# Delta rule and Fourier mixing: unread matrix products between the products of two recurrence steps and behind the first mixed tile

## The chip, the core and the metric

The kernel runs on one core of a Trainium2 chip. TensorE (PE in the profile, its weight loads PEld), VectorE (DVE), ScalarE (ACT) and GpSimd (POOL) each work through a queue of their own in order; SyncE (SP) and POOL issue the DMAs. The metric is the device time of one execution in microseconds (us), lower is better, given as a median of runs. One further execution was taken with the hardware profiler; all rows come from it.

## The reference

Two blocks in a row, all in float32. First a delta rule over 4 batches, 8 heads, 768 steps and a head size of 48:

```
k_n = k / (norm(k) + 1e-6)
for t in range(S):
    y[t]  = q[t] @ state
    v_old = state^T k_n[t]
    state = state + beta[t] * outer(k_n[t], v[t] - v_old)
```

Its output, with the 8 heads side by side (384 columns), is the input x of the second block:

```
mixed = real(fft(fft(x, axis=1), axis=2))
u  = x + mixed
un = (u - mean(u)) / sqrt(var(u) + 1e-6)
out = u + relu(un @ w_ch1) @ w_ch2        # 384 -> 1536 -> 384
```

The weights arrive as float64.

## The kernel before

The recurrence is done in chunks of 64 steps, 12 chunks (`NCH`) to a batch, 48 in all; chunk `m` belongs to batch `m // 12`. A chunk is a call of `chain(m)`, a generator with three stages. The first multiplies the state into the keys (`pc<-st,KQT` in the trace) and lets DVE take the difference `U` from the values; the second applies the chunk's inverted triangle (`pc<-U,wt`), which ACT copies back to `U`; the third adds the chunk to the state (`pc<-U,kp`, then `st<-st,pc` on DVE), and is left out for a batch's last chunk (`if n < NCH - 1`). `outputs` forms the rows of y for a pair of chunks (`py`) and puts them into the tiles `x`, six tiles of 128 rows to a batch, held as three pairs. `prepare` transposes keys and queries (`pt`, then ACT to `KQT`) and forms their products (`pg`); `invert` inverts the triangles on DVE (`A`, `X`), `merge` joins their blocks (`pj`).

`fourier(b)` mixes a batch: `folded` and `shifted` form sums on DVE (`hT`, `F` of the first batch), a product with the table `stab` transforms along the rows (`pf`, read back by ACT into `F` and `gz`), and for each of three tile pairs `T` a product with `dtab` transforms along the columns (`pb`), after which six DVE sums add it to `x[T]`; the last pair has four further sums (`pd`). Mean and variance follow on DVE, the root on POOL (`rstd`). `mlps` normalises (`un`), transposes (`ptr`, `unT`), and does the two products of the last block (`ph`, then ACT to `hT`; `po`, then DVE into `x`).

The float64 weights are turned into float32 on the chip: a DMA brings a tile into one of `x_149`, `x_150`, `x_151` (still free), two ACT passes and two DVE passes split it, and POOL joins it into `w`. The second weight's twelve tiles (`second_weight`) are under way while batch 0 is mixed.

The order of the work is that of the calls, with a planner behind it. Up to `m = 11` the order is written out by hand and kept (`strict[0] = True`). From `m = 12` on it is not: a loop with due times (`PRE`, `SIDE`) mixes `chain`, `prepare`, `invert`, `mlps` and `fourier`, and a scheduler sets the final order on each engine. Results of TensorE go through PSUM tiles. Those that `ps_one` hands out (`pt`, `pf`, `pb`, `pd`, `ph`, `po`, `ptr`) share two slots:

```
def ps_one(shape, name):
    return ps.tile(shape, F32, tag="one", bufs=2, name=name)
```

so each waits until the one two places ahead of it has been read. In the profiled execution chunk 11 begins at 143.7 us, chunk 12 at 154.3 us, and the sums of tile pairs 0, 1 and 2 of batch 0 at 167.4, 178.0 and 187.6 us. A matrix product of the program is two records in the trace. Line 131 in the profile is the helper that issues the calls of DVE, ACT and TensorE, so groups are told apart by tile names.

Of the kernel before, what the change touches and what calls it, by code (L numbers as in the profile page):

```python
# [82 lines left out]
def kernel(  # L83
# [15 lines left out]
    NCH = S // CH  # L99
# [17 lines left out]
    def ps_pair(name, tag):  # L117
        return ps.tile([128, 2, 512], F32, tag=tag, name=name)

    def ps_one(shape, name):  # L120
        return ps.tile(shape, F32, tag="one", bufs=2, name=name)
# [18 lines left out]
    def mm(o, lhsT, rhs, start, stop=True):  # L140
        return pe.matmul(o, lhsT=lhsT, rhs=rhs, start=start, stop=stop, skip_group_check=True)
# [48 lines left out]
    def loads():  # L190


        while at["k"] < min(len(quads), at["chain"] + len(kps)):
            load(at["k"], 0)
        while at["q"] < min(len(quads), at["prepare"] + len(qps)):
            load(at["q"], 1)
# [10 lines left out]
    def values(Q):  # L207
        vals[Q] = wk.tile([128, QT, 4, D], F32, tag="V4", bufs=2, name="V4")
        b, i = quads[Q]
        n = QT * i  # L210
        mid = min(max(NCH // 2 - n, 0), QT)
        for cs in (slice(0, mid), slice(mid, QT)):
            w = cs.stop - cs.start
            t0 = (n + cs.start) * CH + (1 if cs.start < mid else 0)
            for p in range(2):
                for u in range(4):
                    if w:
                        eng = nc.gpsimd if NW <= Q + 1 < 5 and p else nc.sync
                        eng.dma_start(out=vals[Q][64 * p:64 * p + CH, cs, u, :],
                                      in_=v[b, 4 * (p ^ (u % 2)) + u, t0:t0 + w * CH, :].rearrange(  # L220
                                          "(c p) d -> p c d", p=CH))

    def scaled(Q):

        if Q in vals and Q in lengths:
            vf = vals[Q].rearrange("p c u d -> p (c u) d")
            ln = lengths.pop(Q)
            dve.tensor_tensor(vf, vf, ln[:, :, None].broadcast_to([128, QT * 4, D]), op=ALU.mult)
# [11 lines left out]
    stab = const.tile([128, 1281], F32, name="stab")  # L240
# [406 lines left out]
    def first_state(b):  # L647
        xs[b] = [xpairs[i] for i in OF_BATCH[b]]
        v0m = wk.tile([NBH, H, D], F32, tag="un", bufs=2, name="v0m")
        dve.tensor_tensor(v0m, v0[:, None, :].broadcast_to([NBH, H, D]),  # L650
                          ident[0:NBH, H * b:H * b + H, None].broadcast_to([NBH, H, D]), op=ALU.mult)
        p0 = ps_one([128, 2 * 2 * D], "p0")
        for e in range(2):
            mm(p0[64 * e:64 * e + 64], k0, v0m.rearrange("p (j e) d -> p e j d", e=2)[:, e], True)
        dve.tensor_copy(sts[NCH * b % 3].rearrange("p h x -> p (h x)"), p0)

    def chain(m):


        b, n = divmod(m, NCH)  # L660
        Q, c = divmod(m, QT)
        KQT, kp, LQ = held[Q]
        if c == 0:
            scaled(Q)
        V4 = vals[Q]
        wt = wts[Q % NW]
        st, nst = sts[m % 3], sts[(m + 1) % 3]
        if n == 0 and b > 0:
            first_state(b)
        pc = ps_pair("pc", "ch")  # L670

        pk = pc[:, :, 0:2 * D].rearrange("p e (j d) -> p e j d", j=2)
        for j in range(2):
            for hh, e in ((0, 0), (1, 1), (0, 1), (1, 0)):
                pr = slice(64 * e, 64 * e + D)
                o = 64 * (hh ^ e)
                mm(pk[o:o + 64, e, j], KQT[pr, c, j, hh, 0, :], st[pr, hh, D * j:D * j + D], True)
        U = wk.tile([128, 4, D], F32, tag="U", bufs=4, name="U")
        ue = "p (j e) d -> p e j d"
        dve.tensor_tensor(U.rearrange(ue, e=2), V4[:, c].rearrange(ue, e=2), pk, op=ALU.subtract)  # L680
        yield

        pu = pc[:, :, 4 * D:6 * D].rearrange("p e (j d) -> p e j d", j=2)
        for j in range(2):
            for e in range(2):
                for hh in range(2):
                    pr = slice(64 * (hh ^ e), 64 * (hh ^ e) + 64)
                    mm(pu[64 * hh:64 * hh + 64, e, j], wt[pr, c, 2 * j + e], U[pr, 2 * j + e], True)
        act.activation(U.rearrange(ue, e=2), pu, ACT.Copy)
        yield  # L690
        if c == 0:
            at["chain"] = Q
            loads()
            if Q + 1 < len(quads) and Q + 1 not in vals:
                values(Q + 1)
        if c == 1:
            held.pop(Q - 1, None)

        if n < NCH - 1:
            pS = pc[:, :, 2 * D:4 * D]  # L700
            for j in range(2):
                for hh, e in ((0, 0), (1, 1), (0, 1), (1, 0)):
                    pr = slice(64 * hh, 64 * hh + 64)
                    mm(pS[64 * e:64 * e + 64, hh, D * j:D * j + D], kp[pr, c, 2 * j + e, :], U[pr, 2 * j + e], True)
            dve.tensor_tensor(nst, st, pS, op=ALU.add)
        pair[n % 2] = c, KQT, LQ, st, U
        if n % 2 == 1:
            later.append(outputs(b, n, *pair))
        if c == QT - 1:
            scaled(Q + 1)  # L710
        yield
# [65 lines left out]
    def fourier(b):  # L777

        x = xs[b]
# [80 lines left out]
        def add(dst, src, op):  # L860
            dve.tensor_tensor(dst, dst, src, op=op)

        for T in range(TH):
            pb = ps_one([128, DM], "pb")
            ts = slice(128 * T, 128 * T + 128)
            mm(pb[:, 0:HD + 1], F[:, 0, 0, ts], dtab[:, 0, 0:HD + 1], True)
            mm(pb[:, 0:HD + 1], F[0:HD - 127, 0, 1, ts], dtab[0:HD - 127, 1, 0:HD + 1], False)
            mm(pb[:, HD + 1:DM], F[:, 1, 0, ts], dtab[:, 0, HD + 1:DM], False)
            mm(pb[:, HD + 1:DM], F[0:HD - 129, 1, 1, ts], dtab[0:HD - 129, 1, HD + 1:DM], False)
            add(x[T][:, :, 0:HD + 1], pb[:, None, 0:HD + 1].broadcast_to([128, 2, HD + 1]), ALU.add)  # L870
            add(x[T][:, :, HD + 1:DM], pb[:, None, HD - 1:0:-1].broadcast_to([128, 2, HD - 1]), ALU.add)
            for t, op in enumerate((ALU.subtract, ALU.add)):
                rop = ALU.add if op == ALU.subtract else ALU.subtract
                add(x[T][:, t, 1:HD], pb[:, HD + 1:DM], op)
                add(x[T][:, t, HD + 1:DM], pb[:, DM - 1:HD:-1], rop)
            yield
            if T == TH - 1:

                pd = ps_one([128, DM], "pd")
                q3 = slice(96, 128)  # L880
                mm(pd[q3, 0:HD + 1], gz[:, 0, :], dtab[:, 0, 0:HD + 1], True)
                mm(pd[q3, 0:HD + 1], gz[0:HD - 127, 1, :], dtab[0:HD - 127, 1, 0:HD + 1], False)
                for t, op in enumerate((ALU.subtract, ALU.add)):
                    add(x[T][q3, t, 0:HD + 1], pd[q3, 0:HD + 1], op)
                    add(x[T][q3, t, HD + 1:DM], pd[q3, HD - 1:0:-1], op)
                yield
            mv = wk.tile([128, GT, 2], F32, tag="mv", bufs=NC // GT, name="mv")
            for tt in range(GT):
                bst = wk.tile([128, 6], F32, tag="bst", bufs=2, name="bst")
                dve.bn_stats(bst, x[T][:, tt, :])  # L890
                dve.bn_aggr(mv[:, tt, :], bst)
            rstd = wk.tile([128, GT], F32, tag="rstd", bufs=NC // GT, name="rstd")
            pool.tensor_scalar(rstd, mv[:, :, 1], 1e-6, None, op0=ALU.add)
            pool.tensor_tensor(rstd, rstd, half_n, op=ALU.pow)
            norms[b, T] = mv, rstd
            yield
# [129 lines left out]
    M.diagonal(0, 0)  # L1026
    M.products(1, 0)
    step = chain(0)
    advance(step)
    M.diagonal(0, 1, dve.tensor_copy)  # L1030
# [14 lines left out]
    T = lambda l, step: lambda: merges[l].taken(step)  # L1045
# [9 lines left out]
    key_work = {(7, 0): 2, (8, 2): 3, (9, 0): 1, (10, 2): 2, (11, 0): 1, (11, 1): 2, (11, 2): 1}  # L1055
    rest = seq(w.join(), masks(3))
    first_mixing = fourier(0)
    for m in range(1, NCH):
        if m == 3:
            merges.update({2: Merge(1, 0, crossed=False), 3: Merge(1, 1, crossed=False)})  # L1060
        for i, _ in enumerate(chain(m)):
            if pe_work[m][i]:
                pe_work[m][i]()
# [74 lines left out]
    for m in range(NCH, STEPS):  # L1138
        b, n = divmod(m, NCH)
# [70 lines left out]
```

## Time and profile before

| | us |
|---|---|
| median of 6 runs | 776.62 |
| lowest and highest of them | 774.32, 777.77 |
| the profiled execution | 774.29 |
| its span on the core | 772.6 |
| PE busy | 678.4 (88%) |
| DVE busy | 391.1 (51%) |
| ACT busy | 260.9 (34%) |
| POOL busy | 83.3 (11%) |
| mean granted clock of TensorE | 0.982 |

The span is the time between the first and the last record; 1.7 us lie around it. The busy shares say which engine has the most work over the whole, and not which one a stage waits for: for that, the rows of the stage are read in order of time.

### The profile page before, as it was taken

To read this page: it belongs to the slowest core of one execution; us is meant where nothing else is said; L and a number is where in the kernel's file an instruction comes from. 1 tells how busy PE (TensorE), PEld (TensorE's weight loads), DVE (VectorE), ACT (ScalarE), POOL (GpSimd) and SP (SyncE) were. 2 spreads that over 40 slices of the span, in tenths; PEclk is the share of its full clock that TensorE was granted. 3 is DMA by queue.
4 is the path that set the end of the run, shared out by engine and by line. 5 is a ranking of instruction groups with operands and counts; after the bars stand their busy time and mean duration, and the time that the engine had idled before them with its cause. 6 is when DMAs were issued, how large, how long until landed. Compare 5 with 4: busy or idle time off the path is not lost.

```text
span 772.6 us, 18281 instructions
## 1 busy us (share of the span) xinstructions
PE 678.4 (88%) x7768; PEld 487.0 (63%) x7768; DVE 391.1 (51%) x972; ACT 260.9 (34%) x708; POOL 83.3 (11%) x116
## 2 busy tenths in 40 slices
PE   5934598779989989899998999899999989899996
PEld 4622477667647757566756667566667667577683
DVE  2599776877980299436597113989311125300000
ACT  3742354643335512633403445012622021121120
POOL 8010023323100000001100000111000000100000
PEclk9999999998999999999999999899999999999999
DMA  8642033342210221011201110100000000000000
GB/s 185 164 108 47 6 85 64 87 120 68 45 39 17 50 45 31 14 24 38 39 22 30 19 42 3 31 10 17 8 22 2 22 1 1 21 1 21 10 11 20
DMA packets 81041, 30.78 MB, mean 40 GB/s; under 512 B 75856, under 2 KB 77392, under 8 KB 80960
## 3 DMA queue, kind: packets, MB, share of 16 engines
q1 hardware_dynamic: 76560, 21.92, 13.4%
q0 software_dynamic: 2224, 7.31, 3.0%
q8 instruction: 61, 1.00, 0.5%
q10 hardware_dynamic: 2176, 0.39, 0.3%
q14 instruction: 20, 0.16, 0.1%
HBM read 24.87 MB, written 4.72 MB: 38 GB/s over the span
## 4 chain that ended last, share of the span: by engine, by line
PE 54%; DVE 14%; ACT 4%; issue 2%; SPq 1%; DMA 1%; POOL 1%; POOLq 0%; DVEq 0%; ACTq 0%
PE ph L131 20%; PE po L131 18%; DVE X L131 4%; PE pc L131 3%; DVE A L131 3%; PE pf L131 2%; PE pb L131 2%; DVE x L131 2%; ACT wt L131 2%; PE pg L131 2%; PE pt L131 2%; PE py L131 2%; ACT A L131 1%; PE ptr L131 1%; DVE Z L131 1%
## 5 line engine op out<-in xcount | busy, mean ns | idle before, releaser
L131 PE MATMUL ph<-unT,w 128*128 128x256 f32 x864 | 209.0, 391 | 4.3 <-ACT hT L131 2.7
L131 PE MATMUL po<-w,hT 128*128 128x384 f32 x576 | 208.9, 506 | 0.1
L131 PEld LDWEIGHTS ph<-unT,w 128*128 128x128 f32 x864 | 159.1, 191 | 31.2 <-ACT hT L131 5.9
L131 PEld LDWEIGHTS po<-w,hT 128*128 128x128 f32 x576 | 105.4, 193 | 63.3 <-issue 4.2
L131 ACT ACTIVATE hT<-ph 128x256 f32<-128x256 f32 x144 | 54.9, 382 | 187.7 <-PE ph L131 187.2
L131 DVE TENSOR_TENSOR x<-x,po 128x384 f32<-128x384 f32 x24 | 13.2, 550 | 110.2 <-PE po L131 110.2
L131 PE MATMUL pg<-KQT 48*64 48x64 f32 (+1 forms) x1152 | 45.2, 297 | 7.9 <-ACT KQT L131 5.7
L131 PEld LDWEIGHTS pg<-KQT 48*64 48x64 f32 x1152 | 34.4, 178 | 24.3 <-ACT KQT L131 12.7
L770 POOL DMA_INDIRECT out_dram<-x,rows_hi x12 | 12.4, 1030 | 334.8 <-DVE x L131 175.2
L131 DVE TENSOR_TENSOR U<-V,pc 128x192 f32<-128x192 f32 x48 | 16.7, 349 | 57.0 <-PE pc L131 56.9
L131 ACT ACTIVATE KQT<-pt 128x256 f32<-128x256 f32 (+1 forms) x84 | 33.2, 413 | 29.1 <-PE pt L131 28.0
L131 DVE TENSOR_TENSOR A<-X 128x30 f32<-128x30 f32 (+14 forms) x120 | 41.3, 344 | 3.0
L131 ACT ACTIVATE U<-pc 128x192 f32<-128x192 f32 x48 | 15.9, 331 | 79.1 <-PE pc L131 76.8
L131 DVE TENSOR_TENSOR X<-X,A 128x30 f32<-128x30 f32 (+14 forms) x120 | 40.6, 339 | 2.9
L131 DVE TENSOR_TENSOR st<-st,pc 128x192 f32<-128x192 f32 x44 | 15.4, 351 | 43.7 <-PE pc L131 32.0
L131 PEld LDWEIGHTS pc<-st,KQT 48*64 48x64 f32 x768 | 19.3, 158 | 26.6 <-DVE st L131 16.5
L131 PE MATMUL pc<-st,KQT 48*64 48x48 f32 x768 | 26.0, 253 | 10.8 <-DVE st L131 10.5
L131 PEld LDWEIGHTS pc<-U,wt 64*64 64x64 f32 x768 | 20.6, 158 | 20.3 <-issue 9.2
L131 PE MATMUL pt<-pack,qp 128*128 128x128 f32 x96 | 22.6, 331 | 12.2 <-DMA qp<-in_q_dram 11.4
L131 PE MATMUL pc<-U,wt 64*64 64x48 f32 x768 | 27.4, 253 | 5.7 <-DVE U L131 4.1
L131 ACT ACTIVATE A<-pj 32x128 f32<-32x128 f32 (+1 forms) x76 | 20.7, 273 | 32.9 <-PE pj L131 32.2
L131 DVE TENSOR_TENSOR x<-x,pb 128x191 f32<-128x191 f32 (+1 forms) x72 | 24.8, 414 | 13.1 <-PE pb L131 13.0
(135 smaller groups left out, 843.8 us busy)
## 6 DMA issues: line engine op xcount, KB each, us to landing
x<-in_moe_w_ch_dram SPq DMA_DIRECT2D x14, 384.0 KB, 3.4
qp<-in_q_dram SPq DMA_DIRECT2D x96, 48.0 KB, 2.4
kp<-in_k_dram SPq DMA_DIRECT2D x80, 48.0 KB, 2.4
V<-in_v_dram SPq DMA_DIRECT2D x56, 48.0 KB, 2.3
w<-in_moe_w_ch_dram POOLq DMA_DIRECT2D x6, 384.0 KB, 7.7
x<-in_moe_w_ch_dram POOLq DMA_DIRECT2D x4, 384.0 KB, 7.6
V<-in_v_dram SPq DMA_DIRECT2D x64, 24.0 KB, 2.1
out_dram<-x SPq DMA_DIRECT2D x8, 192.0 KB, 1.9
```

Of the source, the lines that this page charges most:

```text
L131: ins = getattr(self.engine, name)(*args, **kwargs)
L770: nc.gpsimd.indirect_dma_start(out=out.rearrange("b s m -> (b s) m"), out_offset=bass.IndirectOffsetOnAxis(ap=rows_hi[:, i:i + 1], axis=0) ...
```

## The change

`busy(m)` issues a product of 128x128 by 128x384 from the table `stab` into a `ps_one` tile named `idle`, that nothing reads. It is called in `chain` behind the first, the second and the third stage, and acts for `m = 11` and `m = 12`. Since the third call stands inside `if n < NCH - 1`, it is not reached for `m = 11`. So five such products are issued. Two further ones stand in `fourier` behind the six sums of batch 0's tile pair 0; they multiply the freshly summed `x[0]` (128 columns of each of its two tiles) with `stab`. Seven in all. No step of the computation is taken out.

```diff
+    def busy(m):
+        if NCH - 1 <= m <= NCH:
+            unread(stab[:, 0:128])
+
+    def unread(lhsT):
+        mm(ps_one([128, 384], "idle"), lhsT, stab[:, 0:384], True)
+
     def chain(m):
...
         dve.tensor_tensor(U.rearrange(ue, e=2), V4[:, c].rearrange(ue, e=2), pk, op=ALU.subtract)
+        busy(m)
         yield
...
         act.activation(U.rearrange(ue, e=2), pu, ACT.Copy)
+        busy(m)
         yield
...
             dve.tensor_tensor(nst, st, pS, op=ALU.add)
+            busy(m)
...
                 add(x[T][:, t, 1:HD], pb[:, HD + 1:DM], op)
                 add(x[T][:, t, HD + 1:DM], pb[:, DM - 1:HD:-1], rop)
+            if b == 0 and T == 0:
+                for t in range(2):
+                    unread(x[T][:, t, 0:128])
             yield
```

In the instruction order that results, TensorE has one `idle` behind chunk 11's `pc<-st,KQT`, one behind its `pc<-U,wt`, two ahead of chunk 12's `pc<-st,KQT` (behind `p<-v0m,k`, the batch's first state), the two that read `x_145` ahead of chunk 13's `pc<-U,wt`, and the last among the `pt` and `ph` of about 200 us. The scheduler also moves other work from about 143 us on. ACT does `x_149`'s second pass ahead of the first `F<-pf` instead of behind the first two, `x_150`'s pair ahead of the last `F<-pf` instead of behind it, and between that `F` and chunk 13's `U<-pc` again three pairs of conversion passes (`x_149`, `x_151` and the next `x_150`, where it had been `x_150`, `x_149`, `x_151`). SP issues one load of `x_150` right behind those of `x_149` and `x_151`, ahead of loads of `kp`. DVE does `X<-X,sm` (one operation of 2.28 us) behind the sums of tile pair 1 instead of ahead of them, and one more pair of conversion passes ahead of the sums of pair 0.

## Prediction

> **What bounds the kernel now.** I read the page first: how busy TensorE is, and the clock it was granted.
>
> ```profile
> span 772.6 us, 18281 instructions
> PE 678.4 (88%) x7768; PEld 487.0 (63%) x7768; DVE 391.1 (51%) x972; ACT 260.9 (34%) x708; POOL 83.3 (11%) x116
> PEclk9999999998999999999999999899999999999999
> ```
>
> PE is the bound over the whole, so seven more products ought to cost time. But the changed place is not typical: slice 10 (174 to 193 us) shows an 8. Windows of 1 us there show the clock falling at 170.8 and returning at 181.0 us; the other changes (331.2, 334.6, 491.6, 498.5, 631.6, 635.0, 658.9, 662.3) lie at whole multiples of 3.41 us from these. So I cut the trace into windows of 3.41 us with that phase (columns: stretch, its length, busy time of PE, PEld, DVE, ACT, POOL with instructions, clock, DMA share, GB/s):
>
> ```profile
> 157.13:160.54 3.41, 3.41 (x30) 3.10 (x30) 2.42 (x10) 0.33 (x1) 0.82 (x1) 1.00 0.62 187
> 167.37:170.78 3.41, 0.37 (x28) 0.24 (x18) 3.41 (x13) 1.59 (x4) 0.00 (x0) 1.00 0.54 193
> 170.78:174.20 3.42, 2.42 (x30) 1.96 (x30) 2.48 (x10) 1.31 (x4) 1.81 (x3) 0.50 0.00 0
> 174.20:177.61 3.41, 3.41 (x18) 2.59 (x16) 3.33 (x5) 0.61 (x2) 2.75 (x3) 0.50 0.32 66
> 177.61:181.02 3.41, 3.41 (x16) 2.10 (x18) 3.30 (x10) 0.14 (x1) 0.99 (x1) 0.50 0.63 193
> 655.47:658.89 3.42, 2.01 (x9) 0.89 (x8) 2.52 (x8) 0.00 (x0) 0.93 (x2) 1.00 0.00 0
> ```
>
> A window in which PE did next to nothing (0.37 of 3.41 us) is followed by 10.2 us at half clock. The last row warns that busy time is not the measure: 2.01 of 3.42 us busy, and the clock fell too. Nor does a full window raise it at once (174.20 was full, the clock came back only after the next).
>
> The clock column has a trap. Ahead of 160.5 us it says 1.00, but durations say half, as the products' rows before 130 us and after 240 us show (min/median/max ns):
>
> ```profile
> L131 PE MATMUL pc<-U,kp x144: 302/304/341, 90.0 to 128.8; 64*64 64x48 f32 x144
> L131 PE MATMUL pc<-U,kp x192: 217/219/254, 243.2 to 394.4; 64*64 64x48 f32 x192
> ```
>
> So the kernel runs cold until 160.5 us, warm for 10 us, cold for 10 us, and then mostly warm.
>
> A measure that fits: weight each record by the share of the 128x128 array it uses (rows x columns in its form), at 0.86 ns a streamed column at full clock (the `po` row below: 24 records of 384 columns from 209.88 to 217.81 us, 0.33 us each) and twice that at half clock. The clock fell after windows with a use of 0.03, 0.33, 0.21, 0.03 and 0.32, and stayed up after 0.35 and more. It rose after 0.71, 0.75 and more, and not after 0.69 and less. I take 0.34 and 0.70 as the two edges.
>
> Now the stage itself, PE and then DVE, in order of time (start, us, engine, operation, count, idle before and who ended it):
>
> ```profile
> 170.78 0.68 PE L131 MATMUL pc<-U,wt 64*64 64x48 f32 x16 [3.04 <-DVE U L131]
> 172.92 1.51 PE L131 MATMUL ptr<-pack,un 128*128 128x128 f32 x6 [0.55 <-DVE un L131]
> 174.76 3.22 PE L131 MATMUL pb<-dtab,F 128*128 128x193 f32 x8
> 177.91 2.93 PE L131 MATMUL ph<-unT,w 128*128 128x256 f32 x6
> 185.90 1.66 PE L131 MATMUL pb<-dtab,F 128*128 128x193 f32 x8
> 187.50 1.56 PE L131 MATMUL ph<-unT,w 128*128 128x256 f32 x6
> 209.88 8.01 PE L131 MATMUL po<-w,hT 128*128 128x384 f32 x24
> ```
> ```profile
> 178.02 2.07 DVE L131 TENSOR_TENSOR x<-x,pb 128x386 f32<-128x386 f32 x6
> 187.60 2.07 DVE L131 TENSOR_TENSOR x<-x,pb 128x386 f32<-128x386 f32 x6 [1.55 <-PE pb L131]
> 191.91 1.19 DVE L131 TENSOR_TENSOR x<-x,pd 32x193 f32<-32x193 f32 x4 [1.40 <-PE pd L131]
> ```
>
> The same eight `pb` records take 3.2 us cold and 1.7 warm, six `ph` 2.9 and 1.6. And DVE waits for them (1.55, 1.40), so this half clock is on the path: the chain of waits goes from `pd` into DVE's sums at 191.9, through the inversion (`A`, `X`) and its loads to 230 us, and only then back to PE.
>
> **The price of one product.** Two records of 0.33 us: 0.66 us warm. Cold: `ph` takes 0.48 us a record (177.98 to 180.84, by the chain) against 0.22 (30 records from 192.27 to 198.85), so up to 2.2 times, 1.3 to 1.45 us.
>
> **Chunk 11's two** stand at 144.2 and about 147.5 us, where PE is cold. The first pushes `py` and `pg` by 1.3 us, of which 1.1 us go into PE's idle time ahead of the second `pg` (at 148.7, ended by ACT). Both cold would leave about 1.5 us, and behind them ACT's `A<-pg`, for which DVE's transpose at 151.6 would wait. But the first product takes the use of the window from 143.5 to 146.9 us from 0.59 to some 0.77: the clock rises at 146.9, and the rest of the batch's end goes warm. I take 0.1 us; bounds -0.3 (DVE has no idle time between 149.4 and 159.5 to give back) and 1.5.
>
> **Chunk 12's two** fill PE's idle 1.91 us ahead of 154.26, ended by `st`. Warm they need 1.3 us, cold 2.6 (0.7 late, but the reader `U` stands on DVE at 156.96 behind sums): 0, at most 0.7. **The last one**, 0.66 us, falls near 200 to 204 us, where PE waits 0.97 us for DVE's `LQ`: 0, at most 0.66.
>
> **The two on x[0]** wait for DVE's sums (167.41 to 169.39; the first half some 0.7 us earlier), so run from about 168.8 to 170.2 in PE's idle 3.04 us. Queued behind them is `pc<-U,wt`, which waits for `U` until 170.7 anyway: 0. Without that idle time they would cost 1.3.
>
> **What the scheduler moves.** ACT does one pass of `x_149` (0.57 us) ahead of the first `F<-pf` and the `x_150` pair (1.0) ahead of the last one; DVE does one pair of passes (0.8) more ahead of pair 0's sums. SP issues `x_150`'s load at 160.4, when its buffer is joined, with `kp` loads behind it. Last, ACT's `U<-pc` of chunk 13 stands behind an `x_150` pair whose load can be issued only when POOL has joined its forerunner (about 168.4) and lands some 3.4 us later: `U` at 172.8 in place of 171.5. PE's second half of `pc<-U,kp` stands behind `ptr`, whose `un` is due at 172.7 with the sums 0.45 us later: so `ptr` goes from 172.9 to 173.2. Cost 0.3 us, bounds 0 and 1.7 (POOL or DMA late).
>
> **The gain.** With the two x[0] products (1.3 us of full use, 0.39 of a window) the window 167.37 goes from 0.03 to 0.42 or more: the clock holds at 170.8. Then `ptr` 173.2 to 173.95, `pc` 0.15, `pb` from 174.1 to 175.7, and pair 1's sums begin at 175.75 in place of 178.02: 2.3 us. From there to the end of the `pd` sums: PE has 36 `ph` records (36 x 0.22 to 0.25, 7.9 to 9.0), 1.6 of `pb`, 0.8 of `pd`, about 1.3 of `pc` and `py`, then DVE 1.2: 13.3 on the mean, so 189.0. DVE has 15.1 us there now (178.02 to 193.11), of which 3.6 idle (0.67, 1.55, 1.40); plus 2.28 of `X<-X,sm`, less 0.8 of passes done earlier, 13.0: 188.8. The later of them, 189.0, stands against 193.1: 4.1 us, less 0.4 for interleaved waits, 3.7. What is late next is DVE's inversion, a queue in fixed order with its loads behind it, so the shift is carried to 230 us and from there by PE to the end. Less 0.1 for chunk 11 (the 0.3 is in already), 3.6 us.
>
> The profiled execution is 774.29 with a span of 772.6; it lies 2.3 us below the median of the runs, near their lowest. I take the saving from the median, less 0.2 for rounding of overlaps: 776.6 - 3.4 = 773.2.
>
> **A rule of the skill.** The Trainium skill, "TensorE: Matmul & The Clock Gate", Part 1, says that a free-running window of about 3.4 us decides, halving the clock after an idle one. The row of 655.47 differs: 2.01 us busy, and it fell. By the page two products would settle the matter, since no window is then idle, and 773.2 would be all but sure; by the rows the next window is open too.
>
> **The rivals.** *One window later.* In the next window, 170.8 to 174.2, the changed order has `ptr` (0.66 us of full use), two small `pc` groups (0.16 each) and a beginning `pb` (0.1): 0.32 of the window, just below the edge. If it falls there, `pb` runs cold (1.5 us lost, 0.6 of the 2.3 left) and the clock is back at 177.6 or 181.0. Back at 177.6, `ph` is warm and 2.2 us remain: 774.4; back at 181.0, 0.5 remain, and with the bounds above 777.0. For it: windows need not lie alike in every run; any that ends between 172.5 and 174.1 holds less than 0.34, 1.6 of 3.41 us, 47%.
>
> *Slower: the first warm-up is spent too early.* Chunk 11's products raise the clock at 146.9, but the idle stretch 152.9 to 156.3 (DVE forms `hT`) drops it at 157.1. The window 157.1 to 160.5 now rises with 0.71, barely. With `pf` begun warm, less of it is left there, some 0.63 by my count: below 0.70 the clock stays half until about 167, and the second group of `pf` (24 records, 162.34 to 165.12) takes 5.3 in place of 2.8 us, ahead of pair 0's sums. Price 2.5 us, decided at a use of 0.70; with no gain behind it 779.1. Against it: the windows of most phases drop it earlier or not at all, and a later warm-up makes a later fall less likely.
>
> *It does not do what it says.* Seven products are issued, not eight; the order shows them. If the clock goes as before for any reason, only the costs are left: 0 to 1, 777.0, together with the late case above.
>
> **How the numbers follow.** The measurement tells about 0.3%, 2.3 us. Clock held: 0.50, of which 0.08 with the marginal windows of 0.33 and 0.32 (331, 659 us) holding as well (1.7 us each, 771). One window later, short: 0.15, half of it beyond 0.3%. No change or late: 0.17. Slower: 0.18. So faster 0.57, same 0.25, slower 0.18. Range 771.0 to 779.0: down to the case with one further window, up to the rival's 779.1; outside lie some 0.2. The likeliest case's own range is 772 to 775.
>
> **What would show it.** Right: clock 1.00 from 170.8 to 181 us, `pb` of pair 1 at 1.7 us, pair 1's sums at 175.8, `pd` sums 4 us earlier, `idle` records of 0.33 us inside PE's idle time. Wrong: a clock of 0.5 from 174 us on; `pf`'s second group near 5 us; DVE's transpose at 151.6 later by more than 1 us; or the shift at 193 us lost again by 230.

## The result, and the profile after

The changed kernel took 772.93 us (median of 35 runs, 768.08 to 778.13) beside 775.62 us before (median of 76, 773.72 to 780.95): 2.7 us less. The ratio, here and below, is one of means, not of medians: 0.9959, 95% interval 0.9945 to 0.9972, so 3.2 us or 0.41% less. It takes the fast runs alone, which leaves out three runs of 801 to 812 us of the two experiments with products at all chunks. The forecast was 773.2 us and a ratio of 0.9956 to the median it started from, 776.62.

The profiled execution of the changed kernel took 768.51 us, near the lowest of its runs, and 5.8 us less than the profiled one of before (774.29). So its profile shows where time went, but more of it than the median has. Its page:

```profile
span 766.8 us, 18308 instructions
PE 677.6 (88%) x7782; PEld 485.2 (63%) x7782; DVE 388.6 (51%) x972; ACT 260.7 (34%) x708; POOL 81.6 (11%) x116
PEclk9999999999999999999999999899999989999999
```

PE has fourteen records more (two to a product) and is busy 0.8 us less in this execution: more was saved by work that ran at full clock than the products took. The 8 of slice 10 is gone.

TensorE in order of time, from ahead of the first mixed tile to `po` (start, us, engine, line, operation, tiles, form, count, idle before and who ended it):

```profile
147.24 1.32 PE L131 MATMUL idle<-stab 128*128 128x384 f32 x2
156.77 1.62 PE L131 MATMUL pf<-stab,hT 128*128 128x65 f32 x14 [1.47 <-DVE hT L131]
158.93 2.50 PE L131 MATMUL pf<-stab,hT 128*128 128x128 f32 x10
162.51 2.86 PE L131 MATMUL pf<-stab,hT 128*128 128x64 f32 x24 [0.55 <-ACT gz L131]
...
168.75 1.85 PE L131 MATMUL idle<-stab,x 128*128 128x384 f32 x4 [0.62 <-DVE x L131]
173.23 0.88 PE L131 MATMUL ptr<-pack,un 128*128 128x128 f32 x6
174.35 1.76 PE L131 MATMUL pb<-dtab,F 128*128 128x193 f32 x8
176.05 1.56 PE L131 MATMUL ph<-unT,w 128*128 128x256 f32 x6
182.07 1.66 PE L131 MATMUL pb<-dtab,F 128*128 128x193 f32 x8
205.59 8.01 PE L131 MATMUL po<-w,hT 128*128 128x384 f32 x24
```

The `pb` of pair 1 takes 1.76 us where it took 3.22, the `ph` behind it 1.56 where it took 2.93. `po` starts at 205.59 instead of 209.88: 4.3 us are carried past DVE's queue. The two `idle` products on x[0] end at 170.60, and chunk 13's `pc<-U,wt` starts at 170.69 as against 170.78 before: they cost nothing there.

DVE's sums of pair 1, the inversion's `X`, and the `pd` sums:

```profile
176.16 2.07 DVE L131 TENSOR_TENSOR x<-x,pb 128x386 f32<-128x386 f32 x6 [0.34 <-PE pb L131]
179.15 1.19 DVE L131 SCALAR_TENSOR_TENSOR X<-X,sm 128x1024 f32<-128x1024 f32 x1
188.07 1.19 DVE L131 TENSOR_TENSOR x<-x,pd 32x193 f32<-32x193 f32 x4 [1.21 <-PE pd L131]
```

They end at 189.26 instead of 193.10.

The clock now goes up at 148.1, down from 158.3 to 161.8, and then stays up until 325.6 us (before: up at 160.5, down from 170.8 to 181.0, down at 331.2). The windows of 3.41 us between those times (stretch, length, busy time of PE, PEld, DVE, ACT, POOL with instructions, clock, DMA share, GB/s):

```profile
154.94:158.35 3.41, 1.94 (x36) 1.70 (x32) 3.41 (x13) 0.00 (x0) 0.45 (x1) 1.00 0.23 39
158.35:161.77 3.42, 3.42 (x43) 3.00 (x42) 1.02 (x6) 1.38 (x4) 0.00 (x0) 0.50 0.90 307
168.59:172.01 3.42, 2.24 (x20) 0.92 (x20) 2.69 (x11) 1.28 (x3) 1.10 (x2) 1.00 0.34 115
172.01:175.42 3.41, 2.46 (x28) 2.01 (x28) 2.94 (x12) 1.77 (x5) 1.41 (x3) 1.00 0.00 0
```

By the prediction's measure their use is 0.32 (the clock falls), 0.55 (it rises again), 0.43 and 0.47 (it stays). The third takes the place of the window that had 0.03 before; the products on x[0] are 1.3 of its 3.41 us (four records of 384 columns at 0.86 ns a column). The second contradicts the edge of 0.70.

### The profile page after: what moved, and what is told of

It is laid out like the page before. It is cut to its first block, busy times and chain, and to the rows that moved or that the text cites. A ratio compares the mean times of both kernels' runs of the same rounds, so it can differ in the third digit from the quotient of the medians.

```text
span 766.8 us, 18308 instructions
## 1 busy us (share of the span) xinstructions
PE 677.6 (88%) x7782; PEld 485.2 (63%) x7782; DVE 388.6 (51%) x972; ACT 260.7 (34%) x708; POOL 81.6 (11%) x116
## 4 chain that ended last, share of the span: by engine, by line
PE 60%; DVE 22%; ACT 8%; issue 3%; DMA 3%; SPq 2%; POOL 1%; POOLq 0%; ACTq 0%; DVEq 0%
PE ph L131 20%; PE po L131 18%; DVE A L131 5%; PE pc L131 5%; DVE X L131 4%; PE pg L131 3%; DVE w L131 3%; PE pf L131 3%; PE pt L131 3%; PE pj L131 3%; ACT wt L131 2%; DVE x L131 2%; ACT A L131 2%; SPq L219 2%; PE pb L131 2%
## 5 line engine op out<-in xcount | busy, mean ns | idle before, releaser
L131 PE MATMUL pc<-st,KQT 48*64 48x48 f32 x768 | 25.6, 250 | 10.2 <-DVE st L131 9.8
L131 PE MATMUL pt<-pack,qp 128*128 128x128 f32 x96 | 22.4, 331 | 13.3 <-DMA qp<-in_q_dram 12.4
L131 ACT ACTIVATE A<-pg 128x256 f32<-128x256 f32 (+1 forms) x72 | 25.4, 378 | 17.0 <-PE pg L131 16.3
```

The lines of the kernel that those rows point to most:

```text
L131: ins = getattr(self.engine, name)(*args, **kwargs)
```

## The experiments

The theory was the prediction's: what counts is the use of the array in each window. The first four kernels ran on one chip beside 29 runs of the kernel before (median 776.60), the other four on another beside 17 (775.61); ratios are to those. The change's own runs were in neither group, and the means of the kernel before differ by 0.12% between the groups, so a difference of 0.1 or 0.2% from the change tells nothing. The shown profile is in each case one execution, and where it lies among the runs is said.

**Only the products on x[0].** In `busy` (the orders on ACT, DVE, POOL and SP are then again those of the kernel before):

```diff
-        if NCH - 1 <= m <= NCH:
+        if False:
```

> Only the two products that read x[0] are left; the five between the steps are out, and the instruction order of ACT is that of before. Theory (the two hold TensorE's clock from 171 to 181 us): clock 1.00 there, sums of pair 1 near 175.8 us, most of the gain kept: 772 to 774 us (2 to 4 us below before). Rival (the five products that warm the clock early, or the order that comes with them, bring the gain): within 1 us of before, 775 to 777.

Measured: 777.18 us (12 runs, 771.42 to 780.79), ratio 0.9985 (0.9955 to 1.0014). The theory's number is missed. Five runs lie at 771.4 to 774.5, where it put all, and seven at 777 to 781. The profiled one took 777.02; PE's second group of `pf` and DVE's sums of pair 0 in it:

```profile
163.78 5.26 PE L131 MATMUL pf<-stab,hT 128*128 128x64 f32 x24 [1.00 <-ACT gz L131]
```
```profile
171.31 2.07 DVE L131 TENSOR_TENSOR x<-x,pb 128x386 f32<-128x386 f32 x6 [1.24 <-PE pb L131]
```

The same two in the kernel before:

```profile
162.34 2.86 PE L131 MATMUL pf<-stab,hT 128*128 128x64 f32 x24 [0.47 <-ACT gz L131]
```
```profile
167.41 2.06 DVE L131 TENSOR_TENSOR x<-x,pb 128x386 f32<-128x386 f32 x6
```

Without the products of chunks 11 and 12 the clock first rises at 170.1 here (the kernel before, which has none either, rose at 160.5 in its profile), so `pf` is cold (5.26 in place of 2.86 us) and the sums are 3.9 us later than before (167.41). The x[0] products then do hold the clock, from 170.1 to 176.9, and it falls one window later, after one with a use of 0.30: the prediction's rival of that name, with `pb` of pair 1 at 2.66 us. So the step products are not mere cost, as the prediction had them: without them the first warm-up is late in this execution, and what x[0] saves is lost ahead of it.

**Only the products of the steps.** Without the two on x[0] (the orders on ACT, DVE, POOL and SP stay those of the change):

```diff
-            if b == 0 and T == 0:
-                for t in range(2):
-                    unread(x[T][:, t, 0:128])
```

> Only the five products between the steps are left; the two on x[0] are out. Theory: the clock rises near 147 us but falls again in the idle time behind the first pair's sums, 3.4 us to 10 us at half from about 170 to 173 us on; 775 to 777.5 us, within 1.5 us of before. Rival (early warm-up or changed order): 772 to 773.5, as the whole change.

Measured: 775.02 us (12 runs, 773.12 to 778.51), ratio 0.9981 (0.9961 to 1.0001), as the theory expected. Its profile (773.12, the fastest of them):

```profile
163.00 5.26 PE L131 MATMUL pf<-stab,hT 128*128 128x64 f32 x24 [0.70 <-ACT gz L131]
...
177.93 2.58 PE L131 MATMUL pb<-dtab,F 128*128 128x193 f32 x8
```
```profile
170.56 2.07 DVE L131 TENSOR_TENSOR x<-x,pb 128x386 f32<-128x386 f32 x6 [1.66 <-PE pb L131]
192.46 1.19 DVE L131 TENSOR_TENSOR x<-x,pd 32x193 f32<-32x193 f32 x4 [1.20 <-PE pd L131]
```

The clock rose at 148.9, fell at 159.1, and came back only at 169.4: this is the prediction's "slower" rival, with pair 0's sums at 170.56, 3.15 us later than before (its price was 2.5). Without the x[0] products it fell again at 172.8, after a window with a use of 0.29; `pb` is cold at its start, and the `pd` sums end at 193.65 (193.10 before). Either half of the change alone gains 0.2% or less, with intervals that include 1; together they gain 0.41%. But both intervals overlap with the change's (0.9945 to 0.9972), so that one half is worth less than both is likely and not shown.

**The same products, narrow.** Same instructions, same order on ACT, DVE, POOL and SP, nearly the same busy time of PE, but on 32x32 of the array:

```diff
-        mm(ps_one([128, 384], "idle"), lhsT, stab[:, 0:384], True)
+        mm(ps_one([128, 384], "idle")[0:32], lhsT[0:32, 0:32], stab[0:32, 0:384], True)
```

> All seven products at their places and with their 384 columns, but of 32 rows by 32 columns of the array in place of 128 by 128, so that TensorE is as long busy with them and ACT, DVE, POOL and SP have the order of the whole change to the instruction; only the array's use by them is a sixteenth. Theory (use of the array, rows times columns, decides on the clock): first rise at 155 us or later, clock falls near 170 us for 7 to 10 us; 775 to 777.5 us. Rival 1 (the changed order brings the gain) and rival 2 (time in which TensorE is busy decides on the clock): both 772 to 773.5 us; rival 2 with the clock at 1.00 from 162 to 181 us, rival 1 with it at 0.5.

Measured: 776.91 us (12 runs, 772.67 to 782.05), ratio 1.0003 (0.9982 to 1.0024), clear of the change's interval: no gain is left that these runs can tell. In the profile (772.67, its fastest), PE and then the window of x[0]:

```profile
169.57 1.69 PE L131 MATMUL idle<-stab,x 32*32 32x384 f32 x4 [0.62 <-DVE x L131]
...
176.08 3.22 PE L131 MATMUL pb<-dtab,F 128*128 128x193 f32 x8
```
```profile
169.35:172.76 3.41, 2.08 (x20) 0.59 (x20) 2.75 (x11) 1.25 (x4) 1.03 (x2) 1.00 0.51 145
```

PE was busy for 2.08 of 3.41 us, hardly less than the 2.24 of the change's window, with a use of 0.07, and the clock fell at 172.8 for 10.2 us; `pb` is back at 3.22. The clock first rose earlier than the theory had it, at 152.3 us and not at 155 or later, but for one window alone: PE was busy in it for 2.79 of 3.42 us, with a use of 0.11, and the clock fell at 155.7. So the gain is neither the scheduler's moves nor PE being busy: it comes from products that use the array. Whether their rows, their columns or their weight loads count was not told apart, since the small products differ in all three. The Trainium skill ("TensorE: Matmul & The Clock Gate", Part 1) halves the clock after an idle window; the window of x[0] here was busy for 61% and it fell.

**Four products on x[0].** The other 128 columns as well:

```diff
                     unread(x[T][:, t, 0:128])
+                    unread(x[T][:, t, 128:256])
```

> Four products on x[0] in place of two, all else as in the change. They fill TensorE until about 171.5 us, 0.8 us beyond the point at which U of chunk 13 is ready, but the next reader, ACT's U, stands behind a load until 172.6 us. Theory (in part of the runs a window that ends between 172.5 and 174 us still drops the clock): fewer such runs, 769 to 772 us. Rival (the two already do all that can be done, and more only delay): 773 to 775.

Measured: 771.39 us (6 runs, 768.35 to 774.11), ratio 0.992 (0.989 to 0.995): in the range of the theory, though the interval overlaps with the change's, so a gain over the change is not shown by this run. In its profile (772.68) the four run at

```profile
169.28 3.15 PE L131 MATMUL idle<-stab,x 128*128 128x384 f32 x8 [0.62 <-DVE x L131]
...
174.80 1.76 PE L131 MATMUL pb<-dtab,F 128*128 128x193 f32 x8
```

The window has a use of 0.79, and the clock holds. Pair 1's `pb` starts 0.45 us later than in the change, but so do the x[0] products (by 0.53): the two further ones delay nothing that is seen here. They are not the only difference, though: from about 174 us on the scheduler gives DVE, ACT, POOL and SP another order than in the change (DVE does conversion passes ahead of chunk 13's `st<-st,pc`, SP a load of `x` ahead of one of `kp`), where the expectation had all else alike. What that order is worth was not tried.

**All steps from chunk 0.** Thirty-three products more (76 `idle` records on `stab` in place of 10; the expectation says 35):

```diff
-        if NCH - 1 <= m <= NCH:
+        if m <= NCH:
```

> The change with the three products per chunk from chunk 0 on (35 more), not only at chunks 11 and 12. Theory: each stands where TensorE waits for DVE's or ACT's answer, so costs little, and the clock is at full from about 90 us on, which takes 0.2 to 0.3 us from each of a chunk's three groups of products on the path, 0.7 us a chunk: 762 to 770 us. Rival: the order up to chunk 11 is written by hand, each product of 0.66 us (1.3 while cold) delays the filler behind it and with it DVE and ACT, by more than the clock gives: 775 to 785 us.

Measured: 789.27 us (6 runs, 786.91 to 812.11), ratio 1.0159 (1.013 to 1.0189); the profiled one took 789.32. The theory fell; the rival had the sign and too small a size. PE in it, then DVE's `U` of chunks 7 and 11, and these two in the kernel before:

```profile
94.41 0.91 PE L131 MATMUL idle<-stab 128*128 128x384 f32 x2
95.25 0.45 PE L131 MATMUL pc<-U,wt 64*64 64x48 f32 x16
95.63 0.91 PE L131 MATMUL idle<-stab 128*128 128x384 f32 x2
```
```profile
129.85 0.35 DVE L131 TENSOR_TENSOR U<-V,pc 128x192 f32<-128x192 f32 x1 [2.16 <-PE pc L131]
160.28 0.35 DVE L131 TENSOR_TENSOR U<-V,pc 128x192 f32<-128x192 f32 x1
```
```profile
121.38 0.36 DVE L131 TENSOR_TENSOR U<-V,pc 128x192 f32<-128x192 f32 x1 [0.80 <-PE pc L131]
145.48 0.35 DVE L131 TENSOR_TENSOR U<-V,pc 128x192 f32<-128x192 f32 x1
```

The clock is full from 93.6 us, and `pc<-U,wt` takes 0.45 us where it took 0.68. But each product stands 0.85 us in line ahead of a record on the chunks' chain, and saves 0.23 there. Nor did the clock stay up, as the theory had it: it was at half again from 120.9 to 131.2 and from 148.2 to 158.5 us. Chunk 11's `U` is 14.8 us later than before, and the span is 15.0 us longer (787.6 against 772.6): the loss was complete by then. Of it 4.3 us arose from chunk 6 to chunk 7 and 5.4 from chunk 9 to chunk 11, around the two cold stretches. With four products on x[0] in the same kernel:

> Products at all chunks from 0 on as in the run with 35 more, and four on x[0]. Theory: 1.5 us below that run, 760 to 768.5 us. Rival: as there, 774 to 784.

Measured: 783.15 us (6 runs, 780.74 to 801.39), ratio 1.0094 (1.0066 to 1.0122), as the rival had it: most of the loss stays. It is less than in the run before it, but that isn't shown to be the work of x[0]: in the profile (780.74, its fastest) pair 0's sums, which come ahead of the products on x[0], already begin 4.3 us earlier (180.20 against 184.50).

**Filling the gap ahead of pf.** In the change the clock still fell at 158.3, after DVE's `hT` had kept PE idle. Two more products at chunk 12's first call (here they come behind its `pc<-st,KQT`):

```diff
+    busied = []
...
         if NCH - 1 <= m <= NCH:
             unread(stab[:, 0:128])
+            if m == NCH and not busied:
+                busied.append(m)
+                unread(stab[:, 0:128])
+                unread(stab[:, 0:128])
```

> The change with two further products behind chunk 12's first group, in TensorE's idle time from 155 to 157 us, where in the profile of the changed kernel the clock fell at 158.3 (window with a use of 0.32). Theory (the fall there is what makes the second group of pf cold in part of the runs, 5.3 in place of 2.9 us): clock at full from 147 us on; fewer runs above 773; median 769 to 772 us. Rival (that fall costs nothing, since the load of x_149 until 160.7 us holds ACT): 772 to 774 us, as the change.

Measured: 772.77 us (12 runs, 768.68 to 776.03), ratio 0.9956 (0.9932 to 0.998): the change's number, so the rival's; 6 of 12 runs lie above 773, against 17 of the change's 35. The fall was removed (in the profile the clock is full from 147.5 to 222.6), and still:

```profile
162.63 2.86 PE L131 MATMUL pf<-stab,hT 128*128 128x64 f32 x24 [1.66 <-ACT gz L131]
```

PE's second group of `pf` begins at 162.63, as in the change (162.51), now after 1.66 us of waiting for ACT's `gz` instead of 0.55. Here a warm `pf` ahead of it bought only idle time.

**The gap and four on x[0] together.**

> Both: two further products in the idle time at 155 us, and four in place of two on x[0]. Theory: hardly a run with a cold stretch between 150 and 185 us; median 768 to 770 us, and a narrower spread than that of the change (10 us). Rival (the spread comes from the later falls near 310, 490 and 630 us): median 771 to 773, spread as before.

Both edits above in one kernel. Measured: 769.38 us (6 runs, 767.66 to 771.07), ratio 0.991 (0.9887 to 0.9933). The interval lies below the change's (0.9945 to 0.9972), so this is faster than both kernels: 6.2 us less than before by the medians. Which of the two edits brings it is open, since neither alone was told from the change, and with the four products comes the other order of the engines (outside TensorE it is the same as with the four alone). The six runs also spread over 3.4 us, where the change's 35 spread over 10; six drawn at random from those 35 lie as close in under 1% of the draws. In the profiled one, the slowest of them (771.07), the clock does fall once in the stage, which the theory hardly expected: at 163.9 after a window with a use of 0.33; it is back at 167.3 and then full up to 310.7.

## Why the prediction was right

**The total.** 3.4 us were predicted; 3.2 were measured between the means, 2.7 between the medians. The order of causes is what the profile shows: x[0]'s window held, and pair 1 ran warm. That the totals agree so well is in part luck. The sum was worked out for one case, the clock held, and the runs are a mixture: 12 of 35 lie at 768 to 770.2 us, 9 at 775 or more, 7 of these above 777, and the profiled one gained 5.8 us. The median of the mixture happens to lie near the sum for the one case. The time of 773.2 was met because two errors cancelled: the saving between the medians was 0.7 us smaller, and the median that the forecast started from, of six runs, lies 1.0 us above that of 76. And the two products on x[0], from which the whole gain was to come, gave a ratio of 0.9985 when they stood alone, with an interval that includes 1.

The steps, in the profile:

- The x[0] products were to run from 168.8 to 170.2 at no cost. They ran from 168.75 to 170.60, at no cost; four records took 1.85 us and not 1.3.
- The scheduler's 0.3: `ptr` was expected at 173.2 and came at 173.23 (before 172.92); ACT's `U` at 172.60 (172.8 expected).
- Pair 1's sums: 176.16, expected 175.75, before 178.02. So 1.9 of the 2.3 us. `pb` began at 174.35 instead of 174.1.
- From there to the end of the `pd` sums 13.1 us, expected 13.3 by PE and 13.0 by DVE; end at 189.26, expected 189.0, so 3.8 us earlier (3.7 expected). The estimate of DVE's side had counted `X<-X,sm` at 2.28 us. It took 1.19, and its sum would have been 1.1 shorter; PE ended last, so nothing followed from it.
- Carried on: `po` 4.3 us earlier, the last `pj` of the inversion 5.1 (225.68 against 230.76), the span 5.8. The last steps are not the stage's: a fall of the clock at 658.9 us is gone in this execution, another at 626.0 lasts 6.8 instead of 3.4 us.

**Chunk 11 and 12: right in cost, with a worth left out.** They were put at 0.1 us and at nothing. DVE's transpose at 151.6 came at 152.08, 0.5 us later and within the bounds, and pair 0's sums at 167.32, 0.1 us earlier than before instead of 0.45 later. But the text gave them no share in the gain. Without them the ratio is 0.9985 (0.9955 to 1.0014) against 0.9959 (0.9945 to 0.9972); since the intervals overlap, a share in the time is likely and not shown. What the profiles show is an earlier warm-up: with the products of 128x128 at chunks 11 and 12 alone the clock first rose between 145.5 and 150.3 us in five of five profiles, without them at 160.5 and 170.1.

**The edge of 0.70 was wrong.** It rested on one trace of before. The clock rose after a use of 0.55 in the change's profile, and in the experiments' after 0.55 to 0.64, and did not after 0.70 to 0.75 in several windows that end between 144 and 160 us. Over all windows of the ten traces, it rose only after ones in which PE was busy for 95% or more, and stayed at half after many as busy; so neither measure tells when it rises. The edge for falls held: in these traces the clock fell only after windows with a use of 0.37 or less and held from 0.33 up, so the two overlap by 0.04. By busy time they would overlap far more: it fell after windows busy for up to 0.81 of their length and held after some busy for 0.46.

**The rivals.** "Slower" happened by half: the clock fell at 158.3 (0.32), so the ten `pf` records at 158.93 ran cold, 2.50 us, but it was back at 161.8 and the second group stayed at 2.86. Had it not come back, `pf` would have taken the 5.26 us that the runs with only one half of the change show. "One window later" did not come in the change's profile: the next window held 0.47, not 0.32, since it began at 172.0 instead of 170.8 and took in 1.1 us of `pb`. It came in that of the x[0]-only kernel. "It does not do what it says" did not come: fourteen `idle` records are in the trace, two to each of the seven products.

**What stays open.** What raises the clock. What it is in a product of 128x128 that holds it and is missing at 32x32. And what share each of the two places has in the median: which executions of the x[0]-only kernel warmed up late is known only for the profiled one.

## What to carry to other kernels

TensorE's idle time can cost twice, by itself and by the clock of what follows: where it waits through a stretch of about 3.4 us, look at what the next 10 us run at, and fill the stretch with products only as far as it is idle anyway. Here products of 128x128 did it and products of 32x32 did not; sizes between were not tried. And the filler must not stand in line ahead of a chain's record: 33 of them cost 15 us there, and the clock fell between them all the same. Look at the neighbouring stages too: holding the clock in one place is worth something only if it has been raised by then.

## What was not expected of the hardware

- Records of `idle` cost more than the warm 0.33 us each: a pair between small products took 0.81 to 0.91 us, four in a row 1.85 to 1.88, eight 3.15. What the surplus of about 0.15 to 0.5 us a group is, was not tried.
- The spread between the change's runs goes with the clock. Those of 768 to 770 us have a mean granted clock of 0.984 to 0.991, those of 773.6 to 774.3 have 0.979, those of 777 to 778 have 0.973 to 0.977. Between 0.986 and 0.973 lie 0.013 x 768 x 2 = 20 us more at half clock, some six windows of 3.41 us, for 9 us of time: about 1.5 us a window. In the x[0]-only kernel it goes so less plainly (772.42 us at 0.977, 777.02 at 0.984); this mean takes the time ahead of the first change for full clock. That an execution is a draw of how its windows lie, and that a kernel with more use in its thin windows has fewer ways to lose, is argued from this.
- The clock column cannot be read ahead of its first change: in the x[0]-only kernel it is 1.00 up to 170.1 us, while `pf` takes 5.26 us there from 163.78 on, against 2.86 warm.
- `X<-X,sm` took 2.28 us before and 1.19 after. In the kernel before POOL had begun an operation 0.12 us ahead of it:

```profile
175.52 1.32 POOL L526 TENSOR_SCALAR_AFFINE_SELECT Y<-sm 128x1024 f32<-128x1024 f32 x1 [0.66 <-DVE sm L131]
```
```profile
175.64 2.28 DVE L131 SCALAR_TENSOR_TENSOR X<-X,sm 128x1024 f32<-128x1024 f32 x1
```

The ten traces agree on it: in the four where POOL's `Y<-sm` had begun 0.1 to 0.3 us earlier, this `X<-X,sm` took 2.27 or 2.28 us and ended 1.06 or 1.07 us behind `Y<-sm`; in the other six, where `Y<-sm` was done, it took 1.19 or 1.20. Near 383 us in the kernel before it is the other way round: DVE begins 0.04 us ahead and takes 1.22 us, and POOL's `Y<-sm` takes 2.31 in place of 1.32. In these rows the later of the two waits for the earlier one; no run changes only this.
